# A two-layer kernel on one core: the second layer's weights prepared during the first layer

## The chip, the cores and the metric

The kernel runs on one core of one Trainium2 chip. The metric is the device time of one execution in microseconds (us). The engines named here are TensorE (PE, matrix products), VectorE (DVE), ScalarE (ACT), and SyncE (SP), which issues the DMAs. Each engine runs its own list of instructions in order, and waits at the head of the list until the inputs of the next instruction are there.

## The reference

A channel attention feeds two feed-forward layers. All data are float32, except that the weights arrive as float64 (the inputs are scaled by a float64 number), so the kernel reads each weight as two 32-bit words and makes a float32 of it itself.

```python
def _attn_ref(q, k, v, tau):            # 1 x 6016 x 256 each
    qn = q / (np.linalg.norm(q, axis=1, keepdims=True) + 1e-06)
    kn = k / (np.linalg.norm(k, axis=1, keepdims=True) + 1e-06)
    s = kn.transpose(0, 2, 1) @ qn / tau
    a = softmax(s)                       # 256 x 256
    return v @ a
def layer1(x, w_in, w_out):              # w_in 256 x 2048, w_out 2048 x 256
    h = x @ w_in
    g = np.where(h > 0.0, h, np.exp(np.minimum(h, 0.0)) - 1.0)
    return g @ w_out
def layer2(x, w_in, w_out):              # the same sizes
    h = x @ w_in
    return (h / (1.0 + np.exp(-h))) @ w_out
```

The softmax is written out in the reference; here it is shortened to a name.

## The kernel before

**Stages.** The first 60 us load q and k, form the 256 x 256 scores and their softmax. The matrix `a` is not applied to v: it is multiplied into the first layer's input weights, so the first layer runs on v itself. Then come the two layers.

**Groups and steps.** The 6016 tokens are 47 tiles of 128, in six groups: five of 8 tiles (1024 tokens) and one of 7. A list `order` (L642) gives the twelve group passes: layer 1 with groups 0 to 5, then layer 2 with groups 0, 5, 1, 2, 3, 4. In the text "pass 0" to "pass 11" are the entries of that list. Each pass has eight steps; a step takes 256 of the 2048 hidden units. In a step `first_a` and `first_b` make the hidden values h (x times `w_in`), `unit` applies the activation function, and `second` multiplies the result g of the step before with `w_out` and adds it up in four PSUM banks y.

**Precision.** A product is three TensorE matmuls (`product`, L263): each operand is split into a high part and a remainder (`split`, L259: a copy on ACT, a subtraction on DVE), and high x high, high x low and low x high are summed.

**Seven or eight block products.** A step's h is a 2 x 2 block matrix (two halves of the hidden units, two halves of the tokens), each block with two halves of the 256 channels. A plain step makes it with eight products, 24 matmuls. The other steps use seven products, 21 matmuls: sums of weight blocks (S1 to S4, `weight_sums`, L369) and sums of input blocks (T1 to T4, in `x_made`, L663) go in, and additions on DVE put the result together from the PSUM banks. Before the change the first pass of each layer is plain (`plain`, L648), passes 0 and 6; its weights are converted while it runs.

**Converting the weights.** `convert` (L378) makes one of eight chunks of a weight matrix: a DMA brings 512 KB to a buffer `st`, ACT makes two passes over the words, DVE four (L387 to L390, called through L244, L247 and L241), then comes the split. For the second layer's `w_in` ("w2i") `weight_sums` adds four DVE additions of 128 columns and one more split. w2i is converted in pass 6 at the start of each step, `w_out` of the layer ("w2o") in the same pass before `second`.

**What orders the work.** All operations are first collected in `ops`; `in_order` (L70) then lists them by a model of the engines in which every operation has a cost and the longest way to the end as its priority. TensorE's own sequence is fixed by the program; on the other engines an operation of low priority is put where the model sees the engine free. Buffers come from rings (`Ring`, L294): three `st` buffers, three `cv`, four `e`, five `h`. So an operation stands where the model put it, and on the chip nothing overtakes it on its engine.

Of the kernel before, what the change touches and what calls it, by code (L numbers as in the profile page):

```python
# [11 lines left out]
F32 = mybir.dt.float32  # L12
F32R = mybir.dt.float32r
# [126 lines left out]
def channel_attention_elu_silu(  # L140
# [54 lines left out]
    small = one.tile([P, 224], F32, tag="small", name="small")  # L195
    wide = one.tile([P, GJ + 2 * MJ, C], F32, tag="wa", name="wide")
    v0 = wide[:, :GJ]
    wo = [one.tile([P, NF, C], F32R, tag=f"wo{a}", name=f"wo{a}") for a in range(2)]
    a21 = one.tile([P, 2, NP, P], F32R, tag="a21", name="a21")
    y_ps = [ps.tile([P, FC], F32, tag=f"y{i}", name=f"y{i}") for i in range(4)]  # L200
    h_ps = [ps.tile([P, FC], F32, tag=f"h{i}", name=f"h{i}") for i in range(4)]
    y_dram = [dram.tile([P, CT, GJ * P], F32, tag=f"yd{i}", name=f"yd{i}") for i in range(NG)]

    def f32(ap):
        return ap.bitcast(F32)
# [34 lines left out]
    def tt(out, a, b, op):  # L240
        do("DVE", width(out.ap), lambda: nc.vector.tensor_tensor(at(out), at(a), at(b), op), [a, b], [out])  # L241
# [11 lines left out]
    def dma(out, src, short=False, by=None):  # L253
        size = 4 * int(np.prod(out.ap.shape))
        n = max(1, size / SPREAD[short] / COST["SP"][0])
        queue, engine = (nc.scalar, "ACT") if by == "ACT" else (nc.sync, "SP")
        do(engine, 0, lambda: queue.dma_start(at(out), at(src)), [src], [out], times=n if engine == "SP" else 2)  # L257

    def split(hi, lo, src):  # L259
        copy(hi, src)  # L260
        tt(lo, src, V(f32(hi.ap), hi.keys), ALU.subtract)
# [44 lines left out]
    def part(v, ap, *what):  # L306
        return V(ap, tuple(v.keys[0]._replace(what=x) for x in what))
# [18 lines left out]
    def wa_at(part, j, a):  # L326

        jj = range(j.start, j.stop) if isinstance(j, slice) else [j]
        aa = range(a.start, a.stop) if isinstance(a, slice) else [a]
        return V(wa[:, part, j, a], tuple(("wa", part, x, y) for x in jj for y in aa))  # L330

    def a21_at(part, j):
        jj = range(j.start, j.stop) if isinstance(j, slice) else [j]
        return V(a21[:, part, j], tuple(("a21", part, x) for x in jj))
# [21 lines left out]
    def load(name, i, *order):  # L356
        src = weights[name].rearrange("(t p) f -> p t f", p=P)
        src = src[:, :, 2 * i * HC : 2 * (i + 1) * HC] if name[-1] == "i" else src[:, 2 * i : 2 * i + 2]
        a, b = src.shape[1], src.shape[2]
        t = sts.take()  # L360
        words = t.ap.bitcast(I32)
        dma(V(words.rearrange("p (a b) -> p a b", a=a), t.keys + order), V(src, ()))
        words = words.rearrange("p (a b w) -> p a b w", a=a, w=2)
        src_of[name, i] = [part(t, words[:, :, :, w], w) for w in range(2)]

    def flat(ap):
        return ap.rearrange("p a b -> p (a b)")

    def weight_sums(s, w0, w1):  # L369

        get = lambda v, i: V(v.ap[:, :, i], v.keys)
        put = lambda i: part(s, s.ap[:, :, i], i)
        tt(put(0), get(w0, 1), get(w1, 1), ALU.add)
        tt(put(1), get(w0, 0), put(0), ALU.subtract)
        tt(put(2), get(w0, 0), get(w0, 1), ALU.subtract)
        tt(put(3), get(w1, 0), put(1), ALU.add)

    def convert(name, i, *order):  # L378
        load(name, i, *order)
        low, high = src_of.pop((name, i))  # L380
        t = cvs.take()
        a, b = low.ap.shape[1:3]
        w = V(t.ap.rearrange("p (a b) -> p a b", a=a), t.keys)
        wi = V(w.ap.bitcast(I32), t.keys)
        copy(w, V(f32(high.ap), high.keys), scale=2.0**-112)
        copy(low, V(low.ap.bitcast(U32), low.keys), scale=2.0**-29)
        ts(w, w, TOP, -TOP, ALU.min, ALU.max)  # L387
        ts(wi, wi, 3, None, ALU.logical_shift_left)
        stt(wi, V(high.ap, high.keys), SIGN, wi, ALU.bitwise_and, ALU.bitwise_or)
        tt(V(flat(wi.ap), wi.keys), V(flat(wi.ap), wi.keys), V(flat(low.ap), low.keys), ALU.add)  # L390
        if name == "w1i":
            s = slice(i % 2 * HC, (i % 2 + 1) * HC)
            hi, lo = (w1i_at(i // 2, a, slice(None)) for a in range(2))
            pieces = [(V(hi.ap[:, :, s], hi.keys), V(lo.ap[:, :, s], lo.keys), w)]
        elif name[-1] == "o":
            pieces = [(wo_at(0, i), wo_at(1, i), w)]
        else:
            pieces = [
                (wa_at(0, i, A11), wa_at(1, i, A11), V(w.ap[:, 0, :P], w.keys)),
                (a21_at(0, i), a21_at(1, i), V(w.ap[:, 0, P:], w.keys)),  # L400
                (
                    *(wa_at(a, i, slice(A12, A22 + 1)) for a in range(2)),
                    V(w.ap[:, 1].rearrange("p (a b) -> p a b", a=2), w.keys),
                ),
            ]
        for hi, _, src in pieces:
            copy(hi, src)
        for hi, lo, src in pieces:
            tt(lo, src, V(f32(hi.ap), hi.keys), ALU.subtract)
        if name == "w2i":  # L410
            h = hs.take()
            s = V(h.ap.rearrange("p (j a b) -> p j a b", j=1, a=4), h.keys)
            two = lambda c: V(w.ap[:, c].rearrange("p (j a b) -> p j a b", j=1, a=2), w.keys)
            weight_sums(s, two(0), two(1))
            split(*(wa_at(a, i, slice(S1, S4 + 1)) for a in range(2)), V(s.ap[:, 0], s.keys))

    with tc.manual_schedule():
        make_identity(nc, ident)
# [228 lines left out]

        def plain(n):  # L648

            return order[n][1] == 0  # L650

        base = [0] * len(order)
        for n in range(1, len(order)):
# [142 lines left out]
        def second(s, u):  # L796
            n, j = steps[s]
            m = cols(n)
            fo, half = u
            f = 2 * j + fo  # L800
            g = g_at.pop((s, u))
            g_free.append(g[0].keys[0][1])
            first_f, last_f = (j, fo) == (0, 1), (j, fo) == (NP - 1, 0)
            w_at = lambda a, c: V(wo[a][:, f, c], (("wo", a, j),))
            if n == final:
                for i in range(TJ):
                    y = y_bank(2 * half + i // 2)
                    product(
                        V(y.ap[:, i % 2 * C : (i % 2 + 1) * C], y.keys),
                        [V(x.ap[:, i * P : (i + 1) * P], x.keys) for x in g],  # L810
                        [w_at(a, slice(None)) for a in range(2)],
                        start=first_f and i % 2 == 0,
                        stop=last_f,
                        skip_group_check=True,
                    )
                return
            for c in range(CT):
                product(
                    cols_of(y_bank(2 * half + c), m),
                    [w_at(a, slice(c * P, (c + 1) * P)) for a in range(2)],  # L820
                    g,
                    start=first_f,
                    stop=last_f,
                )
# [77 lines left out]
        for s in range(len(steps) + 1):  # L902
            prev = s - 1
            now = s < len(steps)
            if now:
                n, j = steps[s]
                if n and j == 0:
                    x_made(n)
                if n == 0 and j % 2 and j < NP - 1:
                    convert("w1i", j + 1)  # L910
                    convert("w1i", j + 2)
                if order[n] == (2, 0):
                    convert("w2i", j)
                first_a(s)
            if s:
                chunk = f"w{order[steps[prev][0]][0]}o", steps[prev][1]
                if plain(steps[prev][0]) and chunk not in EARLY:
                    convert(*chunk)
                second(prev, (1, 1))
                if now:  # L920
                    second(prev, (1, 0))
            if now:
                if n == 0 and j % 2 and j < NP - 1:
                    m_group(j // 2 + 1)
                first_b(s)
            if s:
                second(prev, (0, 1))
                if not now:
                    y_store_final(1)
                    second(prev, (1, 0))  # L930
                second(prev, (0, 0))
                if steps[prev][1] == NP - 1:
                    if steps[prev][0] == final:
                        y_store_final(0)
                    else:
                        y_store(steps[prev][0])
# [36 lines left out]
```

## Time and profile before

| | |
|---|---|
| three runs, us | 1055.42, 1057.75, 1055.51 (median 1055.51) |
| the profiled execution: span, us | 1055.5 |
| PE busy, us (share) | 1042.7 (99%) |
| DVE busy, us (share) | 848.9 (80%) |
| ACT busy, us (share) | 716.0 (68%) |
| DMA, mean | 52 GB/s |

Busy time adds the durations of the instructions and counts overlaps once; on DVE and ACT the duration of an instruction reaches some 70 ns into the next one, so a work sum is better made from the distances between the starts of consecutive instructions. PE's ends are modelled, so for PE too the distances of starts are what to read. "Idle before" an instruction is put down to whatever released it last.

Seen from the trace, pass 0 begins at about 63 us, pass 6 (the first of layer 2) at about 555 us and pass 11 at about 960 us.

### The profile page before, as it was taken

How to read it: one execution, taken by the hardware profiler on the slowest of the kernel's cores; microseconds unless marked ns; L12 is line 12 of the kernel's file. 1: busy time of each engine (PE TensorE's matmuls, PEld its weight loads, DVE VectorE, ACT ScalarE, POOL GpSimd, SP SyncE). 2: the span in 40 equal slices, each digit the busy share in tenths (PEclk: the TensorE clock that was granted, in tenths of full speed). 3: DMA queues.
4: the chain of work that ended last, by engine and by line, in shares of the span. 5: the costliest groups of instructions: out<-in, count | busy, mean ns of one | idle time of the engine just before them, and what ended most of it. 6: DMA issues, size and time to landing. Idle time of an engine off the chain costs nothing.

```text
span 1055.5 us, 13381 instructions
## 1 busy us (share of the span) xinstructions
PE 1042.7 (99%) x4848; PEld 882.5 (84%) x4848; DVE 848.9 (80%) x1432; ACT 716.0 (68%) x1304; POOL 0.8 (0%) x7
## 2 busy tenths in 40 slices
PE   8999999999999999999999999999999999999998
PEld 7778888888888888888998888998888888888997
DVE  6899999999989989989989966667668668657554
ACT  5699988786777777777879845555556455455543
POOL 0000000000000000000000000000000000000000
PEclk9999999999999999999999999999999999999999
DMA  9932241112003003002004303003003003001101
GB/s 348 286 94 60 81 98 62 41 21 60 1 6 74 1 1 75 1 1 80 20 1 140 110 1 75 6 1 76 1 1 80 0 1 80 1 1 23 18 1 40
DMA packets 99602, 54.60 MB, mean 52 GB/s; under 512 B 83024, under 2 KB 84304, under 8 KB 98896
## 3 DMA queue, kind: packets, MB, share of 16 engines
q1 hardware_dynamic: 99440, 53.49, 18.3%
q8 instruction: 38, 0.62, 0.2%
q10 hardware_dynamic: 96, 0.26, 0.1%
q14 instruction: 28, 0.23, 0.1%
HBM read 41.42 MB, written 12.32 MB: 51 GB/s over the span
## 4 chain that ended last, share of the span: by engine, by line
PE 93%; DMA 4%; DVE 1%; SPq 0%; ACT 0%; issue 0%; DVEq 0%
PE y L268 49%; PE h L268 44%; DMA ring<-in_q_dram 2%; DMA wide<-in_q_dram 1%; DMA wide<-in_v_dram 1%; DMA st<-in_moe_w_out_dram 0%; SPq L257 0%; DVE wo L241 0%; DVE cv L247 0%; DVE xs L241 0%; PE h L281 0%; DVE cv L241 0%; PE y L281 0%; PE h L276 0%; DVE cv L244 0%
## 5 line engine op out<-in xcount | busy, mean ns | idle before, releaser
L268 PE MATMUL y<-gs,wo 128*128 128x512 f32 (+1 forms) x2112 | 500.0, 386 | 0.7 <-DVE gs L241 0.7
L268 PE MATMUL h<-xs,wa 128*128 128x512 f32 (+1 forms) x1968 | 472.9, 386 | 0.0
L268 PEld LDWEIGHTS y<-gs,wo 128*128 128x128 f32 x2112 | 395.9, 188 | 76.2 <-DVE e L850 2.7
L268 PEld LDWEIGHTS h<-xs,wa 128*128 128x128 f32 x1968 | 368.0, 188 | 69.4 <-DVE h L241 2.0
L241 DVE TENSOR_TENSOR h<-h,h 128x512 f32<-128x512 f32 (+1 forms) x400 | 269.9, 675 | 78.5 <-PE h L268 69.1
L241 DVE TENSOR_TENSOR gs<-e,gs 128x512 fp32r<-128x512 f32 (+1 forms) x384 | 257.8, 677 | 71.0 <-ACT e L233 67.5
L233 ACT ACTIVATE e<-h 128x512 f32<-128x512 f32 (+2 forms) x385 | 229.8, 600 | 71.7 <-DVE h L241 48.3
L233 ACT ACTIVATE gs<-h 128x512 fp32r<-128x512 f32 (+1 forms) x192 | 117.0, 609 | 159.7 <-DVE h L241 109.8
L247 DVE SCALAR_TENSOR_TENSOR e<-e,h 128x512 f32<-128x512 f32 (+1 forms) x192 | 128.5, 676 | 26.2 <-ACT e L233 25.8
L233 ACT ACTIVATE gs<-e 128x512 fp32r<-128x512 f32 (+1 forms) x192 | 116.6, 614 | 23.0 <-DVE e L247 22.7
L233 ACT ACTIVATE e<-e 128x512 f32<-128x512 f32 (+1 forms) x192 | 117.2, 616 | 2.4
L233 ACT ACTIVATE h<-h 128x512 f32<-128x512 f32 (+1 forms) x80 | 46.3, 579 | 37.4 <-PE h L268 37.1
L241 DVE TENSOR_TENSOR xs<-big,xs 128x512 fp32r<-128x512 f32 (+1 forms) x74 | 48.7, 676 | 2.2 <-ACT xs L233 2.2
L268 PEld LDWEIGHTS y<-wo,gs 128*128 128x128 f32 x384 | 47.9, 192 | 1.1
L268 PE MATMUL y<-wo,gs 128*128 128x256 f32 x384 | 48.3, 283 | 0.0
L233 ACT ACTIVATE xs<-big 128x512 fp32r<-128x512 f32 (+1 forms) x74 | 43.1, 614 | 3.4 <-PE h L268 2.3
L241 DVE TENSOR_TENSOR sums<-sums 128x2048 f32<-128x2048 f32 (+2 forms) x16 | 28.7, 1792 | 10.4 <-ACT sums L233 10.2
L268 PE MATMUL h<-xs,a 128*128 128x512 f32 x96 | 27.3, 392 | 1.1 <-ACT a L233 1.1
L244 DVE TENSOR_SCALAR cv<-cv 128x512 f32<-128x512 f32 (+1 forms) x64 | 26.4, 430 | 1.3 <-ACT cv L233 1.3
L233 ACT ACTIVATE cv<-st 128x512 f32<-128x512 f32 x32 | 21.3, 671 | 7.6 <-DVE h L241 3.2
L276 PE MATMUL y<-ring 128*128 128x256 f32 x92 | 23.6, 415 | 1.7 <-DMA ring<-in_k_dram 1.7
L276 PEld LDWEIGHTS y<-ring 128*128 128x128 f32 x92 | 18.6, 207 | 5.7 <-issue 2.3
(84 smaller groups left out, 376.1 us busy)
## 6 DMA issues: line engine op xcount, KB each, us to landing
st<-in_moe_w_in_dram SPq DMA_DIRECT2D x16, 512.0 KB, 3.8
st<-in_moe_w_out_dram SPq DMA_DIRECT2D x16, 512.0 KB, 3.7
yd<-e SPq DMA_DIRECT2D x20, 256.0 KB, 2.5
big<-yd SPq DMA_DIRECT2D x5, 1024.0 KB, 4.7
out_dram<-big SPq DMA_DIRECT2D x38, 128.0 KB, 2.9
big<-in_v_dram SPq DMA_DIRECT2D x32, 128.0 KB, 3.4
wide<-in_q_dram SPq DMA_DIRECT2D x6, 512.0 KB, 10.0
wide<-in_k_dram SPq DMA_DIRECT2D x6, 512.0 KB, 10.7
```

Of the source, the lines that this page charges most:

```text
L233: nc.scalar.activation(at(out), at(src), func, **{k: at(x) for k, x in kw.items()}, **more)
L241: do("DVE", width(out.ap), lambda: nc.vector.tensor_tensor(at(out), at(a), at(b), op), [a, b], [out])
L244: do("DVE", width(out.ap) / 2, lambda: nc.vector.tensor_scalar(at(out), at(a), at(s1), at(s2), *op), [a, s1, s2], [out])
L247: emit = lambda: nc.vector.scalar_tensor_tensor(at(out), at(a), at(s), at(b), op0, op1)
L268: nc.tensor.matmul(at(out), at(lhs[a]), at(rhs[b]), start=start and a + b == 0, stop=stop and a == 1, **kw)
L276: emit = lambda: nc.tensor.matmul(at(out), at(lhs), at(rhs), start=start, stop=stop, **kw)
```

## The change

The second layer's conversions move. `put_by` (new) converts one chunk of w2i or w2o during passes 1 to 4, one call every second step, sixteen in all; the split is written back into the `st` buffer and sent to a DRAM tile (`wa_dram`, `wo_dram`), for w2i with the sums S1 to S4 as a second buffer and DMA. `take_back` (new) loads a chunk from DRAM into the place in `wa` or `wo` that the last step of layer 1 to read it has left, during pass 5. Pass 6 is no longer plain: it takes seven block products like the passes behind it, with its input sums made in `x_made`. The two `wo` tiles become one, so that one DMA fills both parts.

```diff
-    wo = [one.tile([P, NF, C], F32R, tag=f"wo{a}", name=f"wo{a}") for a in range(2)]
+    wo_both = one.tile([P, 2, NF, C], F32R, tag="wo", name="wo")
+    wo = [wo_both[:, a] for a in range(2)]
+    wa_dram = [dram.tile([P, 2, 7, P], F32, tag=f"wad{i}", name=f"wad{i}") for i in range(NP)]
+    wo_dram = [dram.tile([P, 2, 2, C], F32, tag=f"wod{i}", name=f"wod{i}") for i in range(NP)]
...
+    def put_by(name, i):
+        w, raw = in_f32(name, i)
+        wf = V(flat(w.ap), w.keys)
+        both = V(raw.ap.rearrange("p (a x) -> p a x", a=2), raw.keys)
...
+        split(half(both, 0), half(both, 1), wf)
+        if name == "w2o":
+            dma(V(wo_dram[i].rearrange("p a x r -> p a (x r)"), (("wod", i),)), both)
+            return
+        dma(V(wa_dram[i][:, :, A11], (("wad", i, 0),)), V(blocks(both)[:, :, 0], both.keys))
+        dma(V(wa_dram[i][:, :, A12 : A22 + 1], (("wad", i, 1),)), V(blocks(both)[:, :, 2:], both.keys))
+        t, more = cvs.take(), sts.take()
...
+        weight_sums(V(t.ap.rearrange("p (j a b) -> p j a b", j=1, a=4), t.keys), two(0), two(1))
+        both = V(more.ap.rearrange("p (a x) -> p a x", a=2), more.keys)
+        split(half(both, 0), half(both, 1), t)
+        dma(V(wa_dram[i][:, :, S1:], (("wad", i, 2),)), V(blocks(both), both.keys))
+
+    def take_back(name, i):
+        if name == "w2o":
...
+            dma(V(f32(wo_both[:, :, 2 * i : 2 * i + 2]), keys), V(wo_dram[i], (("wod", i),)))
+        else:
...
+            dma(V(f32(wa[:, :, i]), keys), V(wa_dram[i], tuple(("wad", i, x) for x in range(3))))
...
         def plain(n):
-            return order[n][1] == 0
+            return n == 0
...
-                if order[n] == (2, 0):
-                    convert("w2i", j)
+                if 0 < n < NG - 1 and j % 2 == 0:
+                    at_ = ((n - 1) * NP + j) // 2
+                    put_by(("w2i", "w2o")[at_ % 2], at_ // 2)
                 first_a(s)
...
                 second(prev, (0, 0))
+                if steps[prev][0] == NG - 1:
+                    take_back("w2i", steps[prev][1])
+                    take_back("w2o", steps[prev][1])
```

Counted over the program, TensorE has 24 matmuls of 512 columns fewer, DVE 31 instructions more, ACT 5 fewer, SP 48 DMAs more.

On DVE, in one step in the middle of pass 2, there stood before (`h` are sums of the seven products and their PSUM banks, `e` the activation's values, `gs` the remainders that end a block):

```order
L241 TENSOR_TENSOR h_98<-h_77,h_98 128x512
L241 TENSOR_TENSOR h_99<-h_74,h_98 128x512
L241 TENSOR_TENSOR gs<-e_94,gs 128x512
L241 TENSOR_TENSOR h_99<-h_75,h_99 128x512
L247 SCALAR_TENSOR_TENSOR e_95<-e_95,h_99 128x512
L241 TENSOR_TENSOR h_100<-h_74,h_98 128x512
L241 TENSOR_TENSOR gs<-e_95,gs 128x512
L247 SCALAR_TENSOR_TENSOR e_92<-e_92,h_76 128x512
```

and in the same place now, where `cv` and `st` are the conversion's buffers:

```order
L244 TENSOR_TENSOR h_114<-h_73,h_113 128x512
L244 TENSOR_TENSOR st_102<-cv_104,st_102 128x512
L244 TENSOR_TENSOR h_114<-h_74,h_114 128x512
L247 TENSOR_SCALAR cv_105<-cv_105 128x512
L250 SCALAR_TENSOR_TENSOR cv_105<-st_103,cv_105 128x512
L244 ISA cv_105<-st_103,cv_105 128x1024
L244 TENSOR_TENSOR h_115<-h_73,h_113 128x512
L250 SCALAR_TENSOR_TENSOR e_110<-e_110,h_114 128x512
L250 SCALAR_TENSOR_TENSOR e_107<-e_107,h_75 128x512
```

Four conversion instructions now stand between the additions of a step and the first activation, ahead of the instructions that free PSUM banks for TensorE. Elsewhere too they stand singly and in short runs: 20 of them come as late as pass 5, and the last 7 in the first three steps of pass 6.

On SP, where layer 1 ends, there stood before (`yd` is the layer's output in DRAM, `big` the buffer of a pass's input, `st` a load of weights):

```order
L257 DMA st_87<-in_moe_w_out_dram 128x2x512
L257 DMA st_88<-in_moe_w_out_dram 128x2x512
L257 DMA yd_83<-e_95 128x448
L257 DMA yd_83<-e_92 128x448
L257 DMA yd_83<-e_93 128x448
L257 DMA st_87<-in_moe_w_in_dram 128x2x512
L257 DMA yd_83<-e_94 128x448
L257 DMA big_85<-yd_83 128x2x896
```

and now:

```order
L260 DMA wa<-wad_83 128x2x896
L260 DMA wo<-wod_90 128x2x512
L260 DMA wad_84<-st_103 256x1x128
L260 DMA wa<-wad_84 128x2x896
L260 DMA yd_98<-e_110 128x448
L260 DMA yd_98<-e_107 128x448
L260 DMA yd_98<-e_108 128x448
L260 DMA wod_91<-st_102 128x1024
L260 DMA yd_98<-e_109 128x448
L260 DMA st_102<-in_moe_w_out_dram 128x2x512
L260 DMA wo<-wod_91 128x2x512
L260 DMA big_99<-yd_98 128x2x896
```

The stores of the last layer-1 output now stand behind the load of the last chunk of `wa`, and one of them behind the store of a converted chunk.

## Rows read from the trace of the kernel before

**Rows 1.** The page: span, and the first line of engine busy times.

```profile
span 1055.5 us, 13381 instructions
PE 1042.7 (99%) x4848; PEld 882.5 (84%) x4848; DVE 848.9 (80%) x1432; ACT 716.0 (68%) x1304; POOL 0.8 (0%) x7
```

**Rows 2.** The page: the chain of waits that ended last, by engine.

```profile
PE 93%; DMA 4%; DVE 1%; SPq 0%; ACT 0%; issue 0%; DVEq 0%
```

**Rows 3.** Stretches: length, busy us (instructions) per engine, PE clock, DMA share, GB/s.

```profile
75.00:155.00 80.00, 80.00 (x355) 66.30 (x354) 79.95 (x146) 77.45 (x142) 0.00 (x0) 1.00 0.27 77
155.00:200.00 45.00, 45.00 (x199) 36.61 (x198) 44.55 (x76) 32.91 (x61) 0.00 (x0) 1.00 0.27 71
241.00:323.00 82.00, 82.00 (x361) 67.27 (x360) 74.32 (x120) 61.80 (x113) 0.00 (x0) 1.00 0.12 26
```

**Rows 4.** Timeline of PE, one seven-product step: start, duration, instructions merged.

```profile
200.39 2.20 PE L268 MATMUL h<-xs,wa 128*128 128x512 f32 x9
202.43 2.88 PE L268 MATMUL y<-gs,wo 128*128 128x512 f32 x12
...
210.59 0.62 PE L268 MATMUL h<-xs,wa 128*128 128x512 f32 x2
```

**Rows 5.** Timeline of PE, one plain step of pass 6, first and last row.

```profile
598.93 0.84 PE L268 MATMUL h<-xs,a 128*128 128x512 f32 x3
...
609.81 0.84 PE L268 MATMUL h<-xs,a 128*128 128x512 f32 x3
```

**Rows 6.** Timeline of DVE: where pass 0 and where pass 5 end.

```profile
154.65 1.30 DVE L241 TENSOR_TENSOR gs<-e,gs 128x512 fp32r<-128x512 f32 x2
...
557.91 0.62 DVE L241 TENSOR_TENSOR gs<-e,gs 128x448 fp32r<-128x448 f32 x1
```

**Rows 7.** Timeline of DVE, conversions of pass 6 without a wait.

```profile
581.30 0.28 DVE L241 TENSOR_TENSOR h<-cv 128x128 f32<-128x128 f32 x1
581.50 0.42 DVE L244 TENSOR_SCALAR cv<-cv 128x512 int32<-128x512 int32 x1
581.84 0.29 DVE L241 TENSOR_TENSOR h<-cv,h 128x128 f32<-128x128 f32 x1
582.04 0.68 DVE L241 TENSOR_TENSOR gs<-e,gs 128x512 fp32r<-128x512 f32 x1
582.64 0.69 DVE L241 TENSOR_TENSOR wo<-cv,wo 128x512 fp32r<-128x512 f32 x1
```

**Rows 8.** All waits of 75 to 155 us: who <- whom: total us, times, longest.

```profile
ACT gs L233 <- DVE e L247: 1.1, 3, 0.6
ACT h L233 <- PE h L268: 0.3, 1, 0.3
ACT cv L233 <- DMA st<-in_moe_w_in_dram: 0.3, 1, 0.3
```

**Rows 9.** Waits of DVE from 241 to 323 us (pass 2).

```profile
DVE e L247 <- ACT e L233: 5.5, 6, 1.4
DVE h L241 <- PE h L268: 1.2, 3, 0.5
```

**Rows 10.** Waits over the whole span.

```profile
PEld y L268 <- DVE e L850: 2.7, 10, 0.4
ACT cv L233 <- DMA st<-in_moe_w_out_dram: 2.3, 2, 1.3
ACT cv L233 <- DMA st<-in_moe_w_in_dram: 1.9, 2, 1.6
```

**Rows 11.** The page, costliest groups: busy us, mean ns of one | idle before.

```profile
L233 ACT ACTIVATE e<-h 128x512 f32<-128x512 f32 (+2 forms) x385 | 229.8, 600 | 71.7 <-DVE h L241 48.3
```

**Rows 12.** The page, DMA issues: count, KB each, median us to landing.

```profile
st<-in_moe_w_in_dram SPq DMA_DIRECT2D x16, 512.0 KB, 3.8
yd<-e SPq DMA_DIRECT2D x20, 256.0 KB, 2.5
big<-yd SPq DMA_DIRECT2D x5, 1024.0 KB, 4.7
```

More of the change, by code (lines that the diff above doesn't have):

```diff
@@ L364, in load @@
         src_of[name, i] = [part(t, words[:, :, :, w], w) for w in range(2)]
+        return t
     def flat(ap):
@@ L376, in weight_sums, with in_f32 @@
         tt(put(3), get(w1, 0), put(1), ALU.add)
-    def convert(name, i, *order):
-        load(name, i, *order)
+    def in_f32(name, i, *order):
+        raw = load(name, i, *order)
         low, high = src_of.pop((name, i))
@@ L390, in convert @@
         tt(V(flat(wi.ap), wi.keys), V(flat(wi.ap), wi.keys), V(flat(low.ap), low.keys), ALU.add)
+        return w, raw
+    def convert(name, i, *order):
+        w, _ = in_f32(name, i, *order)
         if name == "w1i":
@@ L394, in convert @@
             pieces = [(V(hi.ap[:, :, s], hi.keys), V(lo.ap[:, :, s], lo.keys), w)]
-        elif name[-1] == "o":
+        else:
             pieces = [(wo_at(0, i), wo_at(1, i), w)]
[L397 to L405, printed above, removed]
         for hi, _, src in pieces:
@@ L409, in convert @@
             tt(lo, src, V(f32(hi.ap), hi.keys), ALU.subtract)
[L410 to L415, printed above, removed]
+    def put_by(name, i):
+        w, raw = in_f32(name, i)
+        wf = V(flat(w.ap), w.keys)
+        both = V(raw.ap.rearrange("p (a x) -> p a x", a=2), raw.keys)
+        half = lambda v, a: V(v.ap[:, a].bitcast(F32R), v.keys)
+        blocks = lambda v: v.ap.rearrange("p a (x r) -> p a x r", r=P)
+        split(half(both, 0), half(both, 1), wf)
[5 more added lines that the diff above has]
+        t, more = cvs.take(), sts.take()
+        two = lambda c: V(w.ap[:, c].rearrange("p (j a b) -> p j a b", j=1, a=2), w.keys)
+        weight_sums(V(t.ap.rearrange("p (j a b) -> p j a b", j=1, a=4), t.keys), two(0), two(1))
[4 more added lines that the diff above has]
+        if name == "w2o":
+            keys = tuple(k for a in range(2) for k in wo_at(a, i).keys)
+            dma(V(f32(wo_both[:, :, 2 * i : 2 * i + 2]), keys), V(wo_dram[i], (("wod", i),)))
+        else:
+            keys = tuple(k for a in range(2) for k in wa_at(a, i, slice(0, 7)).keys)
+            dma(V(f32(wa[:, :, i]), keys), V(wa_dram[i], tuple(("wad", i, x) for x in range(3))))
     with tc.manual_schedule():
@@ L916, in channel_attention_elu_silu @@
                 chunk = f"w{order[steps[prev][0]][0]}o", steps[prev][1]
-                if plain(steps[prev][0]) and chunk not in EARLY:
+                if steps[prev][0] == 0 and chunk not in EARLY:
                     convert(*chunk)
```

## The prediction, made blind

> **What bounds the kernel now.** I read the engine totals first, then the chain of waits, then the stretches, then TensorE's own timeline. In the totals the reader is to see PE at 99% of a span of 1055.5 us and DVE at 80% [rows 1]; in the chain, that PE holds 93% of it and DVE 1% [rows 2]. The stretches show that this is one regime from 75 us to the end: PE is busy in all of every stretch, at the full clock, whether DVE is full (79.95 of 80 us) or not (74.32 of 82) [rows 3]. No row of waits of 75 to 155 us has PE in it at all [rows 8]. So the time of the two layers is a count of matmuls times their distance. A seven-product step has 45 matmuls (21 for h, 24 for y) and lasts from 200.39 to 210.59 us [rows 4]: 10.20 / 45 = 0.2267 us each. A plain step has 48 and lasts from 598.93 to 609.81 us [rows 5]: 10.88 / 48 = 0.2267 us. The two agree, so a plain step has no stall in it that would vanish or stay.
>
> The profiled execution's span is 1055.5 us and the median of the runs is 1055.51, so sums made in the trace can be set against the median without a correction.
>
> **What the change takes off the path.** Pass 6 goes from 48 to 45 matmuls a step: 10.88 - 10.20 = 0.68 us, times 8 steps = 5.44 us. The conversions that leave pass 6 give nothing beyond that, since PE keeps its distance there [rows 5]. Ahead of 75 us and in passes 8 to 11 the instruction lists are the same, and nothing changes.
>
> [...]
>
> **What it adds to DVE, which is the question.** A chunk of w2i costs DVE two scalar operations, two full-width ones for the words, one full-width remainder, four additions of 128 columns and one more remainder; w2o the same without the last five. From start to start a full-width operation takes 0.60 us (582.04 to 582.64), a scalar one 0.34 (581.50 to 581.84), 128 columns 0.20 (581.30 to 581.50) [rows 7]. So w2i: 2 x 0.34 + 4 x 0.60 + 4 x 0.20 = 3.9 us; w2o: 2 x 0.34 + 3 x 0.60 = 2.5 us; eight of each, 51 us. They used to lie in pass 6 and, a few, ahead of it; most now lie in passes 1 to 5.
>
> What room is there? From the last remainder of pass 0 (154.65 us) to that of pass 5 (557.91) 403.3 us go by [rows 6], and PE does not stall in them, so that is also what they may take. I counted DVE's instructions between these two points in both programs and priced them by the distances above (448 columns 0.53, the long transposes 1.0 to 1.13, by width):
> - before, 616 instructions, 358.9 us: 44.4 us free;
> - after, 708 instructions: 52 more of 0.60, 18 more of 0.33 to 0.34, 21 more of 0.20, one of 0.53, together 41.9 us, so 400.8 us: 2.5 us free.
>
> DVE would be 99.4% full for 400 us. That is no loss by itself, but it takes away the reserve: every gap on DVE beyond 2.5 us in all has to come out of PE's time, save what DVE's lag can absorb. The lag is not nothing. In a step, the bank of the first product is complete 0.68 us into the 9 matmuls of `first_b`, and PE writes it again after these 9 and 12 of y, 4.76 us after their start (by 0.2267 each). In between ACT needs two operations of 0.6 us [rows 11] and DVE one of 0.60 [rows 7], 1.8 us, ready at about 2.5 us; some 2 us remain by which DVE may be late before PE sees it.
>
> Bounds of the gaps. From below: 0. From 75 to 200 us DVE is busy 124.5 of 125 us, with conversions mixed in, pass 0 plain and the first steps of pass 1 seven-product, and in the first 80 us of that neither DVE nor PE is among those that wait [rows 3, 8]. An engine that is behind finds its inputs ready. From above: in pass 2 DVE waits 5.5 us for ACT and 1.2 for PE in 82 us [rows 9]; if these 6.7 us stayed as they are through 403.3 us, 33 us of gaps would stand against 2.5 of room, a loss of 30.5 us. The state after is like the first row, full of ready conversions, and not like the second, so I take a value near 0: 0.5 us, for the five ends of passes of layer 1, where PE's weight load waits up to 0.4 us for the copy that empties y, 2.7 us in ten waits [rows 10], and where a late DVE can make that visible.
>
> **The other additions.** ACT gets about 21 us more in the same 403.3 us, from counts at the widths' prices; in pass 2 it is busy 61.80 of 82 us [rows 3], so this fits; if it did not, the two ACT operations in the chain above would eat the 2 us. The DMAs: per chunk of w2i 512 KB in, 896 KB out and 896 KB back, for w2o 512 KB each, some 30 MB in all over 400 us with the weights that only move, where the share of the 16 engines is 0.12 [rows 3]. A chunk lands 3.8 us after its issue and 1 MB from DRAM 4.7 us after [rows 12]; the chunks go back in pass 5 and are read in pass 6, a whole pass later, and the last chunk of w2o, converted in step 2 of pass 6, is wanted in step 7: five steps, 51 us, for two transfers of under 5 us each. The cost is nothing while that distance holds; if one DMA came too late PE would wait for the rest of it, some us. The stores of the last layer-1 output now stand on SP behind a load that waits for PE's last use of `wa`; that use comes before the outputs exist, so nothing is held. One store stands behind the store of a converted chunk, and its `e` buffer is wanted by pass 6's activations: lateness of DVE would be handed on there, 2 us at most by the lag above.
>
> Sum: 1055.5 - 5.44 + 0.5 = 1050.6 us.
>
> **The rivals.**
>
> *DVE eats a part of the gain.* The gaps do not close wholly: waits of ACT and PE operations that the order placed just in time. With a quarter of today's waits left, 8.2 us, less the room of 2.5, PE loses 5.7 us and the time is 1055.7. For it: the order is fixed, so a conversion whose input is late holds the additions behind it. Against: no such wait from 75 to 155 us [rows 8]. Losses of 2.3 to 8.6 us, 1052.3 to 1058.7: chance 0.18.
>
> *DVE becomes the bound of layer 1.* This one ends on the other side. Its place is passes 1 to 5, its price the gaps beyond 2.5 us, and it decides from 5.4 + 2.5 = 7.9 us of gaps on, a quarter of today's waits. With half of them left, 16.5 us, the loss is 14 us and the time 1064.1; with all of them 1080.6. For it: 99.4% full for 400 us has no example in this trace longer than 125 us, and seven-product steps have chains (bank, two ACT operations, DVE, bank) that plain steps have less of. Chance 0.13 for slower by over 0.3%.
>
> *Transfers at the head of a queue.* ACT's pass over the words waits for its load: today 4.2 us in four waits, the longest 1.6, for 32 loads [rows 10]. Sixteen loads now come while DVE and ACT have no reserve, and behind stores on SP that wait for DVE. At today's mean, 0.13 us a load, that is 2.1 us and 1052.7; at 1.6 us for each of the sixteen, 25.6 us and 1076. Against: three `st` buffers and some 25 us from one chunk to the next. Chance 0.06, a third of it within 0.3%. [...]
>
> *The matmuls taken out are worth less than their distance.* If something beside them set the distance of 0.2267 us, a step with three fewer would shorten by less than 0.68 us; at half of it the gain is 2.7 us and the time 1052.8, within 0.3%. Against: the two kinds of step are 0.68 us apart at one distance [rows 4, 5]. Chance 0.01. [...]
>
> That the change does not do what it says I leave out: pass 6's lists have 45 matmuls a step.
>
> **How the numbers follow.** The forecast, 1050.6 with its own range of 1050.0 to 1052.3, has 0.62, a part of the gain lost 0.18, DVE the bound 0.13, late transfers 0.06, the matmuls worth less 0.01. A measurement of this kernel can tell about 0.3%, 3.2 us, from no change. Faster by more: 0.62. Within: 0.18 + 0.02 + 0.01 = 0.21. Slower: 0.13 + 0.04 = 0.17. The range leaves out little below, since nothing gives more than 5.44 us (0.4 us for the runs themselves): 1049.6; above it takes in the second case whole: 1059, with some 0.16 beyond.
>
> **What would show it.** Right: pass 6 steps of 10.20 us; DVE over 97% busy from 155 to 555 us with almost no wait; PE steps of 10.20 us in passes 1 to 4 as before; passes 7 to 11 shifted by 5 us and otherwise equal. Wrong: PE rows waiting for DVE or ACT in passes 1 to 5 and steps over 10.20 us there (DVE the bound), DVE waits for ACT of several us a pass (gaps), ACT or SP waiting for `st` or `wad` (transfers), PE waiting for `wa` or `wo` from DRAM in pass 6.

## The result: slower by 6 us, where 5 us less was forecast

The changed kernel takes 1061.69 us (median of four runs, 1060.9 to 1061.95) against 1055.59 (1055.42 to 1057.75): ratio 1.0055, interval 1.0043 to 1.0067, so slower by over 0.3%. The forecast was 1050.6 with a range up to 1059. One execution of the first kernel of experiment 7 ran at a granted clock of 0.557 and took 1748.64 us; it is left out of that kernel's median and ratio, and its trace, the only one of that kernel, is not read. The page after, its first lines and the chain of waits by engine:

```profile
span 1059.1 us, 13456 instructions
PE 1038.7 (98%) x4824; PEld 874.7 (83%) x4824; DVE 873.7 (82%) x1463; ACT 723.3 (68%) x1299; POOL 0.9 (0%) x7
...
PE 73%; DVE 13%; ACT 5%; DMA 4%; issue 3%; SPq 0%; DVEq 0%; ACTq 0%
```

PE does less work than before (1038.7 us against 1042.7) in a longer span, and its share of the chain falls from 93% [rows 2] to 73%: it waits now. Stretches of the two layers, columns as in [rows 3]:

```profile
155.00:241.00 86.00, 82.48 (x361) 66.77 (x360) 80.95 (x140) 67.75 (x123) 0.00 (x0) 1.00 0.26 75
241.00:323.00 82.00, 80.45 (x352) 65.40 (x351) 81.33 (x140) 67.18 (x123) 0.00 (x0) 1.00 0.25 73
323.00:404.00 81.00, 81.00 (x355) 66.06 (x354) 79.57 (x137) 63.94 (x118) 0.00 (x0) 1.00 0.19 54
404.00:486.00 82.00, 81.54 (x357) 66.22 (x356) 80.67 (x142) 66.03 (x123) 0.00 (x0) 1.00 0.24 68
486.00:558.00 72.00, 70.04 (x335) 61.83 (x334) 68.56 (x130) 55.64 (x114) 0.00 (x0) 1.00 0.59 200
558.00:640.00 82.00, 82.00 (x370) 69.05 (x369) 62.85 (x104) 52.07 (x96) 0.00 (x0) 1.00 0.22 75
```

PE is short in the first two and the fifth, a little in the fourth, and full in the third and the sixth. The clock is 1.00 in all. Pass 6 does what was forecast; two rows of PE there, one seven-product step apart:

```profile
590.31 2.20 PE L271 MATMUL h<-xs,wa 128*128 128x512 f32 x9
...
600.51 2.20 PE L271 MATMUL h<-xs,wa 128*128 128x512 f32 x9
```

10.20 us a step, 0.68 less than [rows 5]. I set the start of each run of y matmuls against the same run in the trace of before; what is lost this way is good to about 0.5 us. Eight steps of pass 6 give 5.44 us back; passes 0 to 5 lose 11.0 us. (Net 5.5; the spans differ by 3.6, because pass 0 starts at 60.81 us here and at 62.71 in the profiled execution of before.) The losses come in lumps (by the times of the kernel before): 0.7 us at 172, 3.15 at 208, 2.0 at 243 to 254, 1.2 at 413 to 418, 0.8 at 484 to 499, 2.4 at 522 to 526. Between 254 and 397 almost nothing is lost, with DVE nearly full (79.57 of 81 us in the third row).

**The lump at 208, read backwards.** PE: start, duration, and in brackets the idle time before, with what ended it:

```profile
201.50 2.88 PE L271 MATMUL y<-gs,wo 128*128 128x512 f32 x12
207.24 3.01 PE L271 MATMUL h<-xs,wa 128*128 128x512 f32 x12 [2.86 <-DVE e L250]
```

PE waits for DVE's instruction of the activation (`e<-e,h`, L250) that reads the h bank last and so frees it. DVE stood still before it:

```profile
198.81 0.42 DVE L247 TENSOR_SCALAR cv<-cv 128x512 int32<-128x512 int32 x1
202.94 0.43 DVE L247 TENSOR_SCALAR cv<-cv 128x512 f32<-128x512 f32 x1 [3.71 <-ACT cv L236]
```

and ACT before that, with the relu and exp (`e<-h`) that DVE and PE wanted queued behind it:

```profile
197.75 0.67 ACT L236 ACTIVATE st<-st 128x512 int32<-128x512 uint32 x1
202.25 0.66 ACT L236 ACTIVATE cv<-st 128x512 f32<-128x512 f32 x1 [3.83 <-DMA st<-in_moe_w_out_dram]
202.81 0.67 ACT L236 ACTIVATE st<-st 128x512 int32<-128x512 uint32 x1
203.37 0.63 ACT L236 ACTIVATE e<-h 128x512 f32<-128x512 f32 x1
```

The load that ACT waited for was issued only at 198.69. SP's queue:

```profile
193.15 0.39 SPq L260 DMA_DIRECT2D st<-in_moe_w_in_dram  x1
193.59 0.51 SPq L260 DMA_DIRECT2D wad<-st  x1
198.69 0.39 SPq L260 DMA_DIRECT2D st<-in_moe_w_out_dram  x1
```

That load reuses the buffer of a 128 KB store issued at 193.59 right behind a 512 KB load. By the program this store was ready when another store of the same buffer went out at 189.39; SP held it behind the load of 193.15, which waited for a buffer of its own. The issue rows (KB, us to landing): that store alone, the load behind it, and for comparison all such stores of 155 to 560 us:

```profile
wad<-st SPq DMA_DIRECT2D x1, 128.0 KB, 5.0
...
st<-in_moe_w_out_dram SPq DMA_DIRECT2D x1, 512.0 KB, 3.5
...
wad<-st SPq DMA_DIRECT2D x8, 128.0 KB, 2.5
```

193.59 + 5.0 = 198.6, then 3.5 for the load: 202.2, and ACT starts at 202.25. ACT was free for this pass at 198.42, before its load was even issued. The order had put the pass where its model of the engines thought the load had landed; nothing overtook it in those 3.83 us, and the `e<-h` behind it starts at 203.37. Over the whole span ACT waits 18.6 us for loads of weights, against 4.2 before [rows 10]; 14.6 of these lie behind 75 us, all for put-by loads, where the kernel before waits 0.6:

```profile
ACT cv L236 <- DMA st<-in_moe_w_in_dram: 10.9, 9, 3.0
ACT cv L236 <- DMA st<-in_moe_w_out_dram: 7.7, 4, 3.8
DVE cv L247 <- ACT cv L236: 6.7, 5, 3.7
```

The lump in pass 5 is the same: a load issued at 522.61, behind stores that stand behind loads back of put-by weights, and ACT idle for it:

```profile
527.17 0.66 ACT L236 ACTIVATE cv<-st 128x512 f32<-128x512 f32 x1 [2.98 <-DMA st<-in_moe_w_in_dram]
```

The lumps at ends of passes lie behind DVE's copies of y (`e L874`, three waits of PE, 2.1 us). So theory A is late transfers; theory B is a DVE that is simply too full.

### The profile page after: what moved, and what is told of

It is laid out like the page before. It is cut to its first block, busy times and chain, and to the rows that moved or that the text cites. A ratio compares the mean times of both kernels' runs of the same rounds, so it can differ in the third digit from the quotient of the medians.

```text
span 1059.1 us, 13456 instructions
## 1 busy us (share of the span) xinstructions
PE 1038.7 (98%) x4824; PEld 874.7 (83%) x4824; DVE 873.7 (82%) x1463; ACT 723.3 (68%) x1299; POOL 0.9 (0%) x7
## 4 chain that ended last, share of the span: by engine, by line
PE 73%; DVE 13%; ACT 5%; DMA 4%; issue 3%; SPq 0%; DVEq 0%; ACTq 0%
PE y L271 37%; PE h L271 33%; DVE h L244 4%; PE y L279 3%; DVE gs L244 3%; ACT e L236 2%; DVE e L250 2%; DMA wad<-st 2%; DMA st<-in_moe_w_in_dram 1%; DMA st<-in_moe_w_out_dram 1%; DMA ring<-in_k_dram 1%; ACT gs L236 1%; DVE cv L244 1%; DVE st L244 1%; ACT xs L236 0%
## 5 line engine op out<-in xcount | busy, mean ns | idle before, releaser
L271 PE MATMUL h<-xs,wa 128*128 128x512 f32 (+1 forms) x1992 | 478.4, 386 | 3.6 <-DVE e L250 3.4
L244 DVE TENSOR_TENSOR h<-h,h 128x512 f32<-128x512 f32 (+1 forms) x440 | 296.5, 674 | 83.2 <-PE h L271 73.7
L250 DVE SCALAR_TENSOR_TENSOR e<-e,h 128x512 f32<-128x512 f32 (+1 forms) x192 | 126.3, 670 | 1.7 <-ACT e L236 1.1
L236 ACT ACTIVATE h<-h 128x512 f32<-128x512 f32 (+1 forms) x88 | 51.1, 581 | 41.9 <-PE h L271 41.8
L236 ACT ACTIVATE st<-cv 128x512 fp32r<-128x512 f32 x24 | 15.0, 625 | 11.3 <-DVE cv L244 11.3
```

Source lines behind the costliest of these rows:

```text
L236: nc.scalar.activation(at(out), at(src), func, **{k: at(x) for k, x in kw.items()}, **more)
L250: emit = lambda: nc.vector.scalar_tensor_tensor(at(out), at(a), at(s), at(b), op0, op1)
L271: nc.tensor.matmul(at(out), at(lhs[a]), at(rhs[b]), start=start and a + b == 0, stop=stop and a == 1, **kw)
```

## The experiments

Losses are PE's in passes 0 to 5, by the same setting of runs of matmuls; ratios are to the kernel before, run on the same chip. Its medians there were 1055.2 to 1056.0, so times of different experiments compare to some 0.8 us; the changed kernel itself was not run again.

**1. Small transfers, same order.** The DMAs of the second layer's weights move 32 columns, which leaves out most of these weights. `less = lambda x: x if cut is None else x[:, :, 0, :cut] if len(x.shape) == 4 else x[..., :cut]`, and in `dma`:

```
-        queue.dma_start(at(out), at(src))
+        queue.dma_start(less(at(out)), less(at(src)))    # cut=32: w2 loads, stores, loads back
```

> The changed kernel with every engine's instructions in the same order, but the DMAs of the second layer's weights (loads, stores to DRAM, loads back) move only 32 columns each, so that the weights of layer 2 are not the right ones. DVE and ACT work as before on full widths. Two theories for the 11.0 us that PE loses in passes 0 to 5. Theory A, late transfers: ACT stands at the head of its queue waiting for a weight load (3.8 us at 198 us, 3.0 at 524 us), and PE's two largest stalls, 3.15 and 2.44 us, follow from it. Theory B, DVE without a reserve: DVE is full and late, whatever the transfers do. A expects ACT's 18.6 us of waits for weight loads to fall under 5, PE's loss to fall to about 5.4 us and the time to about 1056.1; B expects the loss to stay near 11 and the time near 1061.7.

Measured 1050.65, ratio 0.9955 (0.9939 to 0.9971); loss 1.1 us; ACT waits for no such load from 75 to 640 us. That is twice the gain that theory A had expected. DVE is as full as ever in pass 2, where nearly all of the 1.1 us lies:

```profile
241.00:323.00 82.00, 80.94 (x356) 66.19 (x355) 81.35 (x140) 67.27 (x123) 0.00 (x0) 1.00 0.13 29
```

The transfers carry about 10 of the 11 us, and a DVE busy 81.35 of 82 us costs about 1 us when inputs are there. Theory B alone falls.

**2. Thin DVE, same order, whole transfers.** `ap[..., :16]` on the operands of the put-by work on DVE, which leaves out most of that work; the model's costs unchanged.

> The changed kernel with every engine's instructions in the same order and all DMAs whole, but DVE's conversion work for the second layer is done on 16 columns only (the weights of layer 2 are not the right ones). DVE gets some 35 to 40 us of room in passes 1 to 5. Theory B, DVE without a reserve, expects PE's loss to vanish but for some tenths: about 1051. Theory A, late transfers, expects the two ACT waits for loads to stay where the load is late by DMA time alone, and so 1053 to 1056, with the stalls at the ends of passes gone in either case.

Measured 1055.26, ratio 0.9995 (0.9986 to 1.0005); loss 5.8 us. ACT still waits, from 75 to 640 us:

```profile
ACT cv L236 <- DMA st<-in_moe_w_in_dram: 4.1, 3, 3.3
ACT cv L236 <- DMA st<-in_moe_w_out_dram: 3.7, 3, 2.5
```

Not all of the 5.8 us is waits. Behind the stall of pass 5, where PE stood idle for 1.38 and 0.32 us, the granted clock reads 0.50 from 525.10 to 528.40 us, against 1.00 in the four stretches of passes 1 to 4; PE's rows ahead of and in that stretch, and the stretch:

```profile
517.35 2.60 PE L282 MATMUL y<-gs,wo 128*128 128x448 f32 x12
...
524.56 4.06 PE L282 MATMUL y<-gs,wo 128*128 128x448 f32 x11 [0.32 <-DVE gs L253]
...
525.10:528.40 3.30, 3.30 (x10) 2.94 (x9) 3.27 (x7) 2.42 (x5) 0.00 (x0) 0.50 0.10 41
```

The next rows start at 519.78 and 528.45: 11 matmuls take 3.89 us where 12 took 2.43. About 1.6 us are thus the clock's, and some 4.2 of the 11.0 us stay with DVE unburdened, most of the lump of pass 5 and one stall of 1.3 us at the end of pass 1 among them; the expectation had the stalls at ends of passes gone. The rest needs both, late loads and a full DVE. That a full DVE cannot catch up after a stall, and that it makes the stores, and so the next loads, later, are two ways that I argue and have not separated.

**3. Half of the change.** Only `w2i` is put by; `w2o` is converted in pass 6 as before.

```
-            put_by(("w2i", "w2o")[at_ % 2], at_ // 2)
+            if at_ % 2 == 0:
+                put_by("w2i", at_ // 2)
```

> The changed kernel with only w2i put by in passes 1 to 4; w2o is converted straight to its place as before the change, late in pass 5 and in pass 6. Half of the put-by loads and 16 DMAs are gone, DVE's sum for passes 1 to 5 is 396 us in place of 401. Theory A expects about half of the 5.6 us of stalls behind late loads to go, 1058 to 1059, and less if the loads still come right behind stores. Theory B expects the 4.6 us of DVE room to come back one for one, about 1057.

Measured 1055.63, ratio 1.0003 (0.9993 to 1.0013); loss 5.8 us. Half the chunks, half the loss: the gain of pass 6 is just eaten. Both theories had expected more time (1058 to 1059, and 1057), and the change takes work from DVE and from the transfers alike, so it does not tell them apart.

**4. The order expects later loads.** `do(..., more=0.0)` adds `more` to the landing that the model assumes, given as 2.5 us for put-by loads and stores; nothing else in the program changes, and the order is made anew from it.

> The changed kernel with the same work and buffers, but the ordering model counts 2.5 us more until a put-by load or store has landed, so that ACT's pass over the words and all behind it is placed later. Theory A expects the waits of ACT for weight loads to fall from 18.6 us to a few and PE's loss by about 5.6: 1056. Theory B expects only what DVE's fill gives, 398 us in place of 401 in passes 1 to 5: about 1058.7.

Measured 1051.14, ratio 0.996 (0.9945 to 0.9975); loss 0.7 us. Both theories had expected more (1056 and 1058.7). Transfers are whole and DVE is full (81.52 of 82 us busy in pass 2), so neither is the cause by itself; what moved is the order, on ACT, DVE and SP alike. The load of the lump at 208 is an example, on SP and where ACT takes it:

```profile
190.49 1.27 SPq L261 DMA_DIRECT2D wad<-st  x2
193.37 0.39 SPq L261 DMA_DIRECT2D st<-in_moe_w_out_dram  x1
195.48 0.51 SPq L261 DMA_DIRECT2D wad<-st  x1
...
197.20 0.65 ACT L237 ACTIVATE cv<-st 128x512 f32<-128x512 f32 x1
```

Here SP sends the 128 KB store ahead of the loads, as one of the two stores at 190.49; the load goes out at 193.37 in place of 198.69, and ACT takes it with no wait. So the mechanism is the fixed order meeting a late load, and the order that made the load late is SP's as much as ACT's. One late load is left, in pass 6, and PE loses nothing by it, with DVE busy 65.11 of 82 us:

```profile
591.02 0.66 ACT L237 ACTIVATE cv<-st 128x512 f32<-128x512 f32 x1 [2.99 <-DMA st<-in_moe_w_out_dram]
...
558.00:640.00 82.00, 82.00 (x367) 68.48 (x367) 65.11 (x111) 51.57 (x94) 0.00 (x0) 1.00 0.26 86
```

**5. Which transfer.** The cut of experiment 1 on a part of the transfers: the loads alone, the stores and loads back, the loads back alone.

> Every engine's order as in the changed kernel; only the sixteen loads of put-by weights are cut to 32 columns, stores and loads back are whole (the weights of layer 2 are not the right ones). All DMAs cut gave 1050.65. Theory A1, the load's own time is what comes late: a cut load lands 1.7 to 1.9 us after its issue in place of 3.5 to 4.0, and the time goes to 1051 to 1053. Theory A2, the load is issued late because SP first waits for a store to land that frees its buffer: each wait shrinks by some 2 us only, about half of the loss goes, 1055 to 1057.

Measured 1052.92, ratio 0.9972 (0.9963 to 0.9982); loss 3.0 us.

> The complement: loads whole, the stores to DRAM and the loads back cut to 32 columns (the weights of layer 2 are not the right ones). A2 expects the stores to land after 1.9 us in place of 2.4 to 5.0, loads to be issued earlier by as much, and 1051 to 1054; A1 expects the loads to stay late, 1058 to 1060.

Measured 1054.0, ratio 0.9988 (0.9979 to 0.9998); loss 3.6 us.

> Only the loads back in pass 5 are cut to 32 columns; loads and stores are whole (the weights of layer 2 are not the right ones). If the loss of 2.44 us in pass 5 comes from stores and loads that queue behind 896 KB and 512 KB on the same DMA engines, it goes and the rest stays: about 1059. If it comes from the stores alone as in pass 1, nothing changes: 1061.7.

Measured 1057.31, ratio 1.0021 (1.001 to 1.0032); loss 7.6 us: the lump of pass 5 is gone, the lump at 208 stays (2.98 us of PE's time, behind a wait of ACT of 3.76).

The losses fall by 8.0, 7.4 and 3.4 us. The third cut is part of the second; the first two have no DMA in common and yet add up to more than the 11.0 us there are: store, buffer and load are one chain, and shortening either end takes most of it away. The first run lies in the range of theory A1 and the second in that of A2, so how much is a load's own time can't be read from this.

**6. y copied by ACT.** In `y_store` of layer 1 `if c:` becomes `if c and n > 4:`, so that both copies at the ends of passes 0 to 4 are ACT's; once in the changed kernel, once with experiment 4.

> The changed kernel and its ordering model, with both copies that empty y done by ACT in layer 1. At the ends of passes 0 to 4 PE loses some 4.4 us behind DVE's copies. If these stalls are a loss of their own, they go and the time is about 1057.5; if they are the echo of ACT's waits for loads earlier in the pass (all DMAs cut left only 1.1 us of them), the late loads still decide and the new order may lie on either side of 1061, 1056 to 1062.

Measured 1057.77, ratio 1.0016 (1.0007 to 1.0025); loss 6.9 us, 3.0 of it in one stall at 196 us behind a late load. The stalls at ends of passes shrink to 0.2 to 0.6 us each. The time fits both branches of the expectation.

> The kernel with 2.5 us more in the ordering model for put-by DMAs (1051.14), and in layer 1 both copies that empty y are done by ACT and none by DVE: ten copies, 6 us of DVE work, move to ACT, which has some 15 us free a pass. What PE still loses there, about 0.7 to 1 us, stands at the ends of passes behind DVE's copies. If a late DVE is the reason, the time goes down by 0.5 to 1 us, to 1050.3; if ACT, now with both copies in a row, is later than DVE was, it goes up by up to 1 us a pass, 1052 to 1056.

Measured 1052.04, ratio 0.9968 (0.9957 to 0.9979); loss 0.9 us. No better than 4: with loads on time, moving the copies gains nothing. That DVE's copies are a cause of their own is not shown.

**7. More buffers, or more lateness.** `w2o` loads take `tiles["pw"][:, i % 2]`, two 4 KB buffers of their own (alone, and with experiment 4); and experiment 4 with `more=5.0`.

> The changed kernel and its ordering model, with two more 4 KB buffers (the memory of a21, which is free after pass 0) that take the loads of w2o, so that a put-by load no longer waits for the store before it to land. If the loss is the chain store, buffer, load, the loads are on the chip before ACT reaches them, ACT's waits for loads fall under 5 us and the time is 1051 to 1053. If the model's order is at fault wherever the buffers lie (it places ACT's pass as soon as it thinks the load has landed), most of the loss stays: 1057 to 1061.

Measured 1053.6, ratio 0.9979 (0.9969 to 0.9989): between the two ranges expected, nearer to that of the buffers.

> The version the runs point to: 2.5 us more in the ordering model for put-by DMAs and the two more buffers for w2o's loads. Against 1055.5 less 5.44 us it can reach 1050.1; expected 1050.2 to 1051.2, with no wait of ACT for a put-by load over 1 us.

Measured 1052.66, ratio 0.9961 (0.9949 to 0.9974); loss 1.9 us. A miss: the two cures do not add, and the longest wait of ACT for a put-by load is 1.2 us where none over 1 us was expected.

> As the kernel with 2.5 us more in the ordering model for put-by DMAs (1051.14), with 5 us more. If transfers that come late to the head of ACT's queue are the cause, nothing is left to gain from more than they are late by: 1050.3 to 1051.5. If the 1051 came by chance of another order, this third order may lie anywhere between 1051 and 1062.

Measured 1050.64 (1049.88 to 1050.98), ratio 0.9944 (0.9928 to 0.9959); loss 1.0 us: it beats both kernels. Its page, pass 2, and ACT's waits for these loads:

```profile
span 1049.1 us, 13470 instructions
...
241.00:323.00 82.00, 81.88 (x359) 66.54 (x357) 81.65 (x141) 65.80 (x122) 0.00 (x0) 1.00 0.22 59
...
ACT cv L237 <- DMA st<-in_moe_w_in_dram: 0.4, 1, 0.4
```

The same kind of load as in the lump at 208, on SP and where ACT takes it:

```profile
193.28 0.39 SPq L261 DMA_DIRECT2D st<-in_moe_w_out_dram  x1
...
202.78 0.66 ACT L237 ACTIVATE cv<-st 128x512 f32<-128x512 f32 x1
```

9.5 us lie between issue and use, with no wait; in the changed kernel it was 3.6, and all of it a wait. The use stands where it stood (202.78 against 202.25); the issue is 5.4 us earlier, since here too the 128 KB store does not stand behind a load.

## Why the prediction was wrong, step by step

- *Pass 6 saves 5.44 us.* Right, to the row: 10.20 us a step.
- *The matmuls could be worth less.* They are not: three fewer took 0.68 us off a step, 0.2267 each.
- *DVE at 99.4% loses little by itself, 0.5 us taken.* Right in kind, and small if twice the size: 1.1 us in experiment 1, 1.0 in the last one, both with DVE over 81 of 82 us busy in pass 2. The two rivals on DVE, 0.31 of the chance between them, priced gaps that do not appear without late loads. The first of them had named the way, "a conversion whose input is late holds the additions behind it", and priced it from DVE's waits of before, in which no late load stood. What I took for the question was not one by itself; DVE's fullness only raises what late loads cost, 11.0 us against some 4.2 in experiment 2.
- *"The other additions": the cost of the DMAs is nothing while the distance holds.* This step failed. I gave a distance of a whole pass to the transfer back, which is wanted late, and looked at the loads only by their number. For the loads the distance was set by the order's model and by three `st` buffers that now wait for their stores: at 198 us ACT came to its pass 0.27 us before the load was issued, and that load took 3.5. Over passes 0 to 5 this cost PE most of 11.0 us. The remark that one store's lateness would be handed on, "2 us at most", saw such a hold on the wrong buffer, `e`, and not on `st`, where it costs whole loads.
- *The rival of transfers at the head of a queue* was the right mechanism at a chance of 0.06. Its sign, ACT waiting for `st`, came; that of DVE as the bound, PE waiting for DVE, came too, and only experiment 1 tells them apart. Its size came from today's mean, 0.13 us a load; measured are 14.6 us of waits behind 75 us, 0.9 us for each of the sixteen new loads, between that mean and its upper end of 1.6. "Three `st` buffers and some 25 us from one chunk to the next" was no argument: the buffer came free when the store had landed (193.59 + 5.0 = 198.6, the load issued at 198.69), not when the chunk was due. ACT took nothing ahead of its pass over the words: at 198 it stood idle for 3.83 us with the relu and exp queued behind. With DVE as full as it was (80.95 of 86 us busy from 155 to 241 us, 3.71 of the rest in one wait behind this load), the lateness of that one load so became 3.15 us of PE's.
- *The base.* The span of 1055.5 us is not the whole time: the execution after has a span of 1059.1 and took 1060.9. By the same 1.8 us the profiled execution of before took some 1057.3, and was one of the longer ones. The sum stood on the median's figure all the same, so this moved nothing.

With the loads on time the forecast time is met: 1050.64 in the last kernel of experiment 7, against 1050.6 (and 1050.65 in experiment 1, which leaves out most of the transfers).

## What to carry to other kernels

Work moved to a place where an engine is full cost little here once its inputs were there (1.1 us in experiment 1, 1.0 in the last kernel of experiment 7, DVE over 81 of 82 us busy in pass 2); ask first, for each load that an engine's next instruction waits for, when its buffer comes free, which store ahead of it decides that, and what that store stands behind on its own queue. A fixed order built on a model that takes landings too early turned one late transfer into idle time of ACT (3.83 us), DVE (3.71) and PE (2.86) in the lump at 208; giving the model 5 us of margin cost nothing that these runs show and was worth 11 us (1061.69 against 1050.64). The mean wait read from the kernel with slack, 0.13 us a load, was no price for the same transfers without it: 0.9 us.

## What the runs showed of the hardware

The 128 KB stores `wad<-st` landed after 2.2 to 2.8 us, but after 5.0, 4.1 and 4.4 us where a 512 KB load had been issued on the same queue at most 1.2 us ahead (193.59, 518.41 and 556.70 us in the changed kernel), 1.5 to 2.3 times as long. In the last kernel of experiment 7 DVE ran 398.05 of 404 us, five passes, with PE at 403.51:

```profile
152.00:556.00 404.00, 403.51 (x1806) 336.63 (x1805) 398.05 (x693) 326.19 (x612) 0.00 (x0) 1.00 0.30 91
```
